# Wider rows in a routing table, a shorter start for VectorE, a store behind weight loads, and two PSUM banks for one pair

## Chip, cores, metric

The kernel runs on one core of a Trainium2 chip. The metric is the device time of one execution in microseconds. TensorE multiplies matrices, VectorE and ScalarE work on what it leaves in PSUM, GpSimd (POOL) makes masks and indices and issues some transfers, and SyncE (SP) issues most of them.

## What is computed

Three layers follow one another: attention with a local window and 32 global tokens, a routed layer of eight experts, and a dense gated layer on all 2176 tokens.

```python
s_ll = scale * np.matmul(q_l, k_l.transpose(0, 1, 3, 2))
s_ll = np.where(np.abs(pos[:, None] - pos[None, :]) <= 32, s_ll, -1000000000.0)
s_l = np.concatenate([s_lg, s_ll], axis=-1)       # 512 local queries, 32 global keys
out_l = np.matmul(sm(s_l), np.concatenate([v_g, v_l], axis=2))
out_g = np.matmul(sm(s_g), v_all)                 # 32 global queries see all keys
...
do_compute = x @ w_skip > 0                       # the others keep x
e_idx = np.argmax(xc @ w_gate, axis=1)
y[mask] = gate_w[mask, None] * (np.maximum(xc[mask] @ w1[e], 0.0) @ w2[e])
out[do_compute] = xc + y
...
return ((x @ w_a) * (x @ w_b) @ w_out).astype(np.float32)
```

There are 4 batches of 8 heads of size 64; the model width is 512, an expert's inner width 1024, the dense layer's 1536. All is float32.

## The kernel before

**Attention** (to some 131 us of the trace) works on 16 pairs of heads, four to a batch. `pair(p)` issues, on every engine, pieces of several pairs: scores S of pair p+2 (`emit_S`, `sps`), their masked maxima M on VectorE (`emit_M`, tiles `sm` and `nm`), exponentials E on ScalarE (L986), transposes T of the next pair (`tps`, `tpg`, copied to `pt`, `ptg`), values PV of pair p (`emit_PV`, into `o`), then X (`emit_X`): the copy `ot` of `o` is multiplied by `xi`, an identity with the router's weights beside it, back into the same PSUM tile `o`, and VectorE writes the token rows `xt` and the logits `lg`. A `slot` may bring a step of the global queries (`emit_G`: `gps`, `gtp`, `gop`); the table `GSTEPS` says in which slots. `pend` holds transfers, and each `tick` after a group of matmuls lets one be issued: keys and queries (`raw`), values (`vt`), stores of `x2d`, sixteen writes of zeros to `xs` (`zero_xs`), and the first weights of the experts. `start()` issues S, M and E of pairs 0 and 1 and T of pair 0, with `idle(n)` putting n matmuls on constants (`zp<-zb`) between them. `last_pairs` is the end of it, pairs 14 and 15, in which the experts' first steps already begin.

**Routing.** Every token gets a slot in the table `xs` in DRAM, 256 rows and more for each expert; a row is 512 floats of the token, a gate weight and the token's number, `ROW` = 514 floats. POOL scatters the rows of `xt` (four tiles a batch) and of `xg` (the global tokens) by an indirect transfer. Rows that no token fills keep what `zero_xs` wrote. `load_row` reads 128 rows of `xs` for an expert.

**Experts** (132 to 276 us) go through the work items of `WORK`, four steps to each. A step needs two loads of weights of 512 KB (`fetch(i)`: a part of `w1` and one of `w2`, tiles `raw`), which ScalarE and VectorE split into a high and a low part (`hi`, `lo`); `layer1` makes `ph`, ScalarE's `hr` is turned in `turn_h` (`pt`), `layer2` sums into `acc`. All weights, rows and stores of `x2d` are issued by SP in one order, written out below L1600: weights of steps 4 to 6, then `st.store_last()` (the four stores of the last batch's tokens), then `st.fetch(7)`, then the rows of the third item, and from there weights seven steps ahead.

**The dense layer** (276 to 690 us) adds its result up in the output; the last tile is done in two halves of 256 columns, each stored as soon as VectorE has it (L560).

Of the kernel before, what the change touches and what calls it, by code (L numbers as in the profile page):

```python
# [27 lines left out]
ROW = 514  # L28
REG = NTOK
# [26 lines left out]
          (2, 0): (32, 37, 38), (2, 1): (40, 45, 46), (3, 0): (43, 49, 54), (3, 1): (48, 53, 57)}  # L56
# [8 lines left out]
def moe_stack_kernel(ctx: ExitStack, tc: tile.TileContext, qk, v, gq, w9, w1, w2, wa, wb, wo, out):  # L65
# [5 lines left out]
    xs = dram.tile([E * REG, ROW], F32, name="xs")  # L71
# [17 lines left out]
class State:  # L89
# [66 lines left out]
    def load_row(self, k, t, xr, scat):  # L156
        r = self.tc.nc.sync.dma_start(xr, self.xs[bass.ds(self.expert(k) * REG + 128 * (WORK[k][1] + t), 128), :])
        after(self.tc, r, scat)
# [92 lines left out]
class Late:  # L251
# [286 lines left out]
    def second(self, b, g):  # L538

        nc = self.nc  # L540
        for q, t in enumerate(self.TILES[b]):
# [8 lines left out]
            for c in halves:  # L550
# [7 lines left out]
                if g == self.NM // 2 - 1:  # L558
                    nc.vector.tensor_tensor(o[:, c], acc[:, c], o[:, c], ALU.add)
                    nc.sync.dma_start(dst[:, c], o[:, c])  # L560
# [265 lines left out]
def attention_and_routing(tc, const, ident, qk, v, gq, w9, x2d, xs, st_):  # L826
    nc = tc.nc
    with ExitStack() as st:
# [14 lines left out]
        xg = c1.tile([128, ROW], F32, name="xg")  # L843
# [11 lines left out]
        zrow = c1.tile([128, ROW], F32, name="zrow")  # L855
# [64 lines left out]
        nc.gpsimd.memset(masks[64:128, 2, 96:128], -1e30)  # L920
        nc.gpsimd.memset(zrow, 0.0)
# [19 lines left out]

        nc.vector.tensor_copy(xg[:, 513:514].bitcast(I32), tokid[:, 16:17])
        nc.vector.tensor_copy(base, pb8)
# [73 lines left out]
        def emit_PV(p):  # L1017

            o = oxs[p] = ps_o.tile([128, 2, 512], F32, tag="o", name="o")
            vt = vts[p]  # L1020
            for j in range(2):
                for k in range(2):
                    r = slice(64 * k, 64 * k + 64)
                    for hh in range(2):
                        c = slice(64 * hh, 64 * hh + 64)
                        mm = nc.tensor.matmul(o[c, k, 128 * j:128 * j + 128], lhsT=vt[r, WIN, c], rhs=pts[p, 2][r, j, :],
                                              start=(j == 0), stop=False, skip_group_check=True)
            tick(mm)
            for i in range(4):
                k, j = divmod(i, 2)  # L1030
                for w in range(2):
                    c = slice(64 * w, 64 * w + 64)
                    for hh in range(2):
                        r = slice(64 * hh, 64 * hh + 64)
                        mm = nc.tensor.matmul(o[r, k, 128 * j + 64 * w:128 * j + 64 * w + 64], lhsT=vt[:, 2 * i + w, r],  # L1035
# [4 lines left out]
            st_.ot = nc.scalar.activation(ot.rearrange("p k j q -> p k (j q)"), o[:, :, 0:256], AF.Copy).ins  # L1040
# [9 lines left out]
        def emit_X(p):  # L1050
            b, hp = divmod(p, 4)
            if hp == 0:
                xt[b] = x_p.tile([128, 4, ROW], F32, tag="xt", name="xt")
                lg[b] = r_p.tile([128, 4, 6, 9], F32, tag="lg", name="lg")
                lgp[b] = r_p.tile([128, 4, 3, 9], F32, tag="lgp", name="lgp")
            o, ot = oxs.pop(p), ots.pop(p)
            for k in range(2):
                for j in range(2):
                    mm = nc.tensor.matmul(o[:, k, 146 * j:146 * j + 146], lhsT=ot[:, k, j, :], rhs=xi[:, hp, :], start=True, stop=True)  # L1059
            tick(mm)  # L1060
            xp = o[:, :, 0:292].rearrange("p k (j h c) -> p k j h c", j=2, h=2)
            ld = lg[b][:, :, 2 * hp:2 * hp + 2, :] if hp < 3 else lgp[b][:, :, 1:3, :]
            nc.vector.tensor_tensor(ld.rearrange("p (k j) h e -> p k j h e", k=2), xp[:, :, :, :, 64:73],
                                    dens[p][:, :, :, :, None].to_broadcast([128, 2, 2, 2, 9]), ALU.mult)
# [7 lines left out]
            def tokens():  # L1072
                nc.vector.tensor_tensor(
                    xt[b][:, :, 128 * hp:128 * hp + 128].rearrange("p (k j) (h d) -> p k j h d", k=2, h=2),
                    xp[:, :, :, :, 0:64],
                    dens[p][:, :, :, :, None].to_broadcast([128, 2, 2, 2, 64]), ALU.mult)
# [296 lines left out]
        def start():  # L1373
            nc.vector.memset(xi[0:64, :, 73:146], 0.0)
            nc.vector.memset(xi[64:128, :, 0:73], 0.0)
            for hp in range(4):
                nc.vector.tensor_copy(xi[0:64, hp, 0:64], ident[0:64, 0:64])
                nc.vector.tensor_copy(xi[64:128, hp, 73:137], ident[64:128, 64:128])
# [5 lines left out]
            nc.scalar.dma_start(w9s, w9.rearrange("a p e -> p a e"))  # L1384
            for g in gpts:
# [13 lines left out]
            idle(4)  # L1399
            emit_T(0)  # L1400
            emit_M(1, 1)

# [9 lines left out]
def experts(tc, const, dram, ident, w1, w2, x2d, xs, st, late):  # L1412
    nc = tc.nc
    with ExitStack() as es:
# [190 lines left out]
        for i in range(4, 7):  # L1605
            st.fetch(i, (1,) if i < 6 else (0, 1))
        st.store_last()
        st.fetch(7)
# [224 lines left out]
```

## Time and profile before

| | |
|---|---|
| time, median of 3 runs | 704.7 us (703.27 to 707.7) |
| the profiled execution, as timed | 698.71 us |
| its span, first to last instruction | 696.9 us |
| TensorE busy | 674.1 us, 97% |
| VectorE, ScalarE, POOL busy | 490.6, 397.0, 130.8 us |
| mean granted TensorE clock | 0.996 |
| DMA | 154.86 MB, 222 GB/s in the mean |

The span is what the trace covers; the timed figure of the same execution has 1.8 us around it. The median of the timed runs lies 6 us above that execution, so a stretch read from the trace counts as a difference, not as a share of the median. [...] Busy times are sums over stages that differ: attention waits for vectors, scalars and transfers, the two later stages for TensorE.

### The profile page before, as it was taken

To read this page: it belongs to the slowest core of one execution; us is meant where nothing else is said; L and a number is where in the kernel's file an instruction comes from. 1 tells how busy PE (TensorE), PEld (TensorE's weight loads), DVE (VectorE), ACT (ScalarE), POOL (GpSimd) and SP (SyncE) were. 2 spreads that over 40 slices of the span, in tenths; PEclk is the share of its full clock that TensorE was granted. 3 is DMA by queue.
4 is the path that set the end of the run, shared out by engine and by line. 5 is a ranking of instruction groups with operands and counts; after the bars stand their busy time and mean duration, and the time that the engine had idled before them with its cause. 6 is when DMAs were issued, how large, how long until landed. Compare 5 with 4: busy or idle time off the path is not lost.

```text
span 696.9 us, 16731 instructions
## 1 busy us (share of the span) xinstructions
PE 674.1 (97%) x6329; PEld 604.6 (87%) x6329; DVE 490.6 (70%) x1278; ACT 397.0 (57%) x973; POOL 130.8 (19%) x213
## 2 busy tenths in 40 slices
PE   8898999989999999999999999999999999999996
PEld 5777887868998888879999999999999999999995
DVE  5667878986968999967975796856375656544444
ACT  5667778865857884567467554544454544443220
POOL 4002213130101210010111122312231232212000
PEclk9999999999999999999999999999999999999999
DMA  8898778799999936632785589996599679549853
GB/s 282 219 233 281 240 222 280 229 310 361 371 369 346 346 121 228 219 134 92 226 333 128 77 188 327 313 221 119 65 268 216 121 151 327 75 61 213 288 179 111
DMA packets 86141, 154.86 MB, mean 222 GB/s; under 512 B 8663, under 2 KB 40279, under 8 KB 84516
## 3 DMA queue, kind: packets, MB, share of 16 engines
q1 hardware_dynamic: 69236, 110.80, 49.1%
q0 software_dynamic: 15744, 42.87, 27.5%
q8 instruction: 52, 0.85, 0.5%
q14 instruction: 37, 0.30, 0.1%
q10 hardware_dynamic: 1072, 0.04, 0.1%
HBM read 105.95 MB, written 51.18 MB: 225 GB/s over the span
## 4 chain that ended last, share of the span: by engine, by line
PE 80%; ACT 3%; DMA 3%; DVE 3%; issue 1%; POOL 0%; SPq 0%; DVEq 0%; POOLq 0%
PE bank L527 32%; PE bank L557 19%; PE acc L1516 8%; PE ph L243 6%; PE bank L583 3%; DMA raw<-w 3%; PE ph L235 2%; PE o L1059 1%; PE sps L963 1%; PE bank L462 1%; PE pt L1502 1%; ACT sm L986 1%; PE o L1035 1%; PE tps L1000 1%; PE tp L204 1%
## 5 line engine op out<-in xcount | busy, mean ns | idle before, releaser
L527 PE MATMUL bank<-xh,w 128*128 128x256 f32 (+1 forms) x1232 | 251.4, 290 | 0.1
L527 PEld LDWEIGHTS bank<-xh,w 128*128 128x128 f32 x1232 | 200.5, 189 | 4.2 <-DVE tmp L649 0.4
L527 PE MATMUL bank<-xl,w 128*128 128x256 f32 (+1 forms) x616 | 178.4, 290 | 0.0
L557 PE MATMUL bank<-woh,g 128*128 128x512 f32 (+1 forms) x412 | 143.7, 392 | 1.2 <-ACT o L563 0.5
L527 PEld LDWEIGHTS bank<-xl,w 128*128 128x128 f32 x616 | 116.1, 188 | 4.2
L181 DVE TENSOR_TENSOR lo<-raw,hi 128x1024 fp32r<-128x1024 f32 x72 | 87.0, 1221 | 11.9 <-ACT hi L171 10.8
L557 PEld LDWEIGHTS bank<-woh,g 128*128 128x128 f32 x412 | 77.3, 188 | 15.6 <-ACT o L563 1.0
L557 PE MATMUL bank<-wol,g 128*128 128x512 f32 (+1 forms) x206 | 80.4, 390 | 0.0
L171 ACT ACTIVATE hi<-raw 128x1024 fp32r<-128x1024 f32 x72 | 75.4, 1054 | 7.8 <-PE acc L1516 4.4
L607 ACT ACTIVATE g<-tmp 128x256 fp32r<-128x256 f32 (+1 forms) x88 | 37.8, 431 | 69.7 <-DVE tmp L649 68.9
L564 POOL DMA_DIRECT2D out<-raw x48 | 39.1, 815 | 141.6 <-ACT raw L563 127.0
L639 DVE TENSOR_TENSOR tmp<-bank,tmp 128x256 f32<-128x256 f32 (+1 forms) x44 | 18.8, 440 | 58.5 <-PE bank L527 58.4
L563 ACT ACTIVATE raw<-bank 128x512 f32<-128x512 f32 x48 | 28.6, 595 | 51.6 <-PE bank L557 50.5
L986 ACT ACTIVATE sm<-sm,nm 128x160 f32<-128x160 f32 x128 | 52.9, 419 | 7.8 <-DVE nm L975 7.8
L564 POOL DMA_DIRECT2D out<-o x37 | 29.6, 801 | 139.2 <-ACT o L563 101.7
L607 ACT ACTIVATE tmp<-bank 128x256 f32<-128x256 f32 (+1 forms) x88 | 34.6, 400 | 25.7 <-PE bank L527 22.2
L649 DVE TENSOR_TENSOR tmp<-bank,tmp 128x256 f32<-128x256 f32 (+1 forms) x88 | 38.9, 442 | 11.7 <-PE bank L527 10.2
L557 PEld LDWEIGHTS bank<-wol,g 128*128 128x128 f32 x206 | 38.7, 188 | 4.6
L645 DVE TENSOR_TENSOR g<-tmp,g 128x256 fp32r<-128x256 f32 (+1 forms) x88 | 38.3, 437 | 3.1 <-ACT g L607 1.4
L563 ACT ACTIVATE o<-bank 128x512 f32<-128x512 f32 x37 | 21.9, 596 | 31.9 <-PE bank L557 29.9
L243 PE MATMUL ph<-hi,xh 128*128 128x256 f32 x132 | 40.0, 303 | 0.0
L243 PE MATMUL ph<-hi,xl 128*128 128x256 f32 x132 | 37.5, 284 | 0.0
(265 smaller groups left out, 1276.5 us busy)
## 6 DMA issues: line engine op xcount, KB each, us to landing
raw<-w SPq DMA_DIRECT2D x64, 512.0 KB
out<-raw POOLq DMA_DIRECT2D x48, 256.0 KB, 4.6
out<-o POOLq DMA_DIRECT2D x37, 256.0 KB, 4.5
raw<-qk SPq DMA_DIRECT2D x28, 272.0 KB
xr<-x2d SPq DMA_DIRECT2D x25, 256.0 KB
raw<-wa SPq DMA_DIRECT2D x12, 512.0 KB
raw<-wb SPq DMA_DIRECT2D x12, 512.0 KB
raw<-wo SPq DMA_DIRECT2D x12, 512.0 KB
```

What stands on the lines that cost most here:

```text
L171: nc.scalar.activation(hi, rv, AF.Copy)
L181: nc.vector.tensor_tensor(lo, rv, hi.bitcast(F32), ALU.subtract)
L243: nc.tensor.matmul(ph, lhsT=x[:, d, :], rhs=w[:, d, :], start=(z == 0), stop=(z == 11))
L527: self.nc.tensor.matmul(bank[:, 0:n], lhsT=w[:, k], rhs=x[:, xp, k], start=start and z == 0, stop=z == 5, skip_group_check=not start)
L557: nc.tensor.matmul(acc[:, c], lhsT=a, rhs=w[:, c], start=(j == 0 and z == 0), stop=(j == 1 and z == 2))
L563: nc.scalar.activation(o, acc, AF.Copy)
L564: i = nc.gpsimd.dma_start(dst, o, accum_op=ALU.add if g else ALU.bypass)
L607: cp = lambda o, i: nc.scalar.activation(o, i, AF.Copy)
L645: tt(g4[2 * j + 1][:, h], (u, p)[h][j], g4[2 * j].bitcast(F32)[:, h], ALU.subtract)
L649: tt(v, (b1, b2)[h][j][:, 0:n], v, ALU.mult)
L986: st_.exp = nc.scalar.activation(sm, sm, AF.Exp, bias=nm[:, hh, j:j + 1], scale=-1.0, accum_out=dens[p][:, k, j, hh:hh + 1]).ins
L1516: nc.tensor.matmul(acc, lhsT=a[:, j, c], rhs=w[:, j, :], start=(q == 0 and z == 0), stop=(q == NQ - 1 and z == 5))
```

## The change

Six edits are made at once.

Rows of `xs` are 528 floats apart (`PITCH`) in place of 514; the zero row, `xg` and `xt` are as wide, with the pad filled on POOL, and `load_row` still reads 514 floats of each row. In `start()` eight copies into `xi` go from VectorE to ScalarE, two copies that read POOL's token numbers go behind the maxima of pair 1, and `idle(4)` is left out. `st.store_last()` is issued behind `st.fetch(7)`. PV of pair 14 writes two tiles of one bank each from the pool of the score tiles, and its copies and products are split in two. One global step's transposes, of (3, 0), move from slot 49 to slot 51, from before the values of pair 12 to before its X. The last tile's second half is stored from ScalarE's queue.

```diff
--- before.py
+++ after.py
@@ -26,6 +26,7 @@
 ROW = 514
+PITCH = 528
 REG = NTOK
@@ -53,7 +54,7 @@
 GSTEPS = {(0, 0): (3, 5, 6), (0, 1): (8, 13, 14), (1, 0): (16, 21, 22), (1, 1): (24, 29, 30),
-          (2, 0): (32, 37, 38), (2, 1): (40, 45, 46), (3, 0): (43, 49, 54), (3, 1): (48, 53, 57)}
+          (2, 0): (32, 37, 38), (2, 1): (40, 45, 46), (3, 0): (43, 51, 54), (3, 1): (48, 53, 57)}
@@ -68,7 +69,7 @@
     x2d = dram.tile([NTOK, DM], F32, name="x2d")
-    xs = dram.tile([E * REG, ROW], F32, name="xs")
+    xs = dram.tile([E * REG, PITCH], F32, name="xs")
@@ -154,7 +155,7 @@
     def load_row(self, k, t, xr, scat):
-        r = self.tc.nc.sync.dma_start(xr, self.xs[bass.ds(self.expert(k) * REG + 128 * (WORK[k][1] + t), 128), :])
+        r = self.tc.nc.sync.dma_start(xr, self.xs[bass.ds(self.expert(k) * REG + 128 * (WORK[k][1] + t), 128), 0:ROW])
         after(self.tc, r, scat)
@@ -557,7 +558,7 @@
                     nc.vector.tensor_tensor(o[:, c], acc[:, c], o[:, c], ALU.add)
-                    nc.sync.dma_start(dst[:, c], o[:, c])
+                    (nc.scalar if c.start else nc.sync).dma_start(dst[:, c], o[:, c])
             if g < self.NM // 2 - 1:
@@ -840,7 +841,7 @@
-        xg = c1.tile([128, ROW], F32, name="xg")
+        xg = c1.tile([128, PITCH], F32, name="xg")
         sp = c1.tile([128, NT, 18], F32, name="sp")
@@ -852,7 +853,7 @@
         masks = c1.tile([128, 3, 160], F32, name="masks")
-        zrow = c1.tile([128, ROW], F32, name="zrow")
+        zrow = c1.tile([128, PITCH], F32, name="zrow")
         gq_sb = c1.tile([128, B, H, SG], F32, name="gq_sb")
@@ -918,6 +919,7 @@
         nc.gpsimd.memset(masks[64:128, 2, 96:128], -1e30)
+        nc.gpsimd.memset(xg[:, ROW:], 0.0)
         nc.gpsimd.memset(zrow, 0.0)
@@ -938,9 +940,6 @@
             nc.gpsimd.iota(tokid[32 * b:32 * b + 32, NT - 1:NT], pattern=[[0, 1]], base=b * (SL + SG), channel_multiplier=1)
-
-        nc.vector.tensor_copy(xg[:, 513:514].bitcast(I32), tokid[:, 16:17])
-        nc.vector.tensor_copy(base, pb8)
@@ -1016,14 +1015,19 @@
-            o = oxs[p] = ps_o.tile([128, 2, 512], F32, tag="o", name="o")
+            if p == NPAIR - 2:
+                both, o = None, [ps_s.tile([128, 512], F32, tag="s", name="o2") for k in range(2)]
+            else:
+                both = ps_o.tile([128, 2, 512], F32, tag="o", name="o")
+                o = [both[:, k] for k in range(2)]
+            oxs[p] = both, o
             vt = vts[p]
...
                         c = slice(64 * hh, 64 * hh + 64)
-                        mm = nc.tensor.matmul(o[c, k, 128 * j:128 * j + 128], lhsT=vt[r, WIN, c], rhs=pts[p, 2][r, j, :],
+                        mm = nc.tensor.matmul(o[k][c, 128 * j:128 * j + 128], lhsT=vt[r, WIN, c], rhs=pts[p, 2][r, j, :],
                                               start=(j == 0), stop=False, skip_group_check=True)
@@ -1032,12 +1036,17 @@
                         r = slice(64 * hh, 64 * hh + 64)
-                        mm = nc.tensor.matmul(o[r, k, 128 * j + 64 * w:128 * j + 64 * w + 64], lhsT=vt[:, 2 * i + w, r],
+                        mm = nc.tensor.matmul(o[k][r, 128 * j + 64 * w:128 * j + 64 * w + 64], lhsT=vt[:, 2 * i + w, r],
                                               rhs=pts[p, hh][:, i, c], start=False, stop=True, skip_group_check=True)
...
             ot = ots[p] = ot_p.tile([128, 2, 2, 128], F32, tag="ot", name="ot")
-            st_.ot = nc.scalar.activation(ot.rearrange("p k j q -> p k (j q)"), o[:, :, 0:256], AF.Copy).ins
+            of = ot.rearrange("p k j q -> p k (j q)")
+            if both is None:
+                for k in range(2):
+                    st_.ot = nc.scalar.activation(of[:, k], o[k][:, 0:256], AF.Copy).ins
+            else:
+                st_.ot = nc.scalar.activation(of, both[:, :, 0:256], AF.Copy).ins
@@ -1050,18 +1059,21 @@
             if hp == 0:
-                xt[b] = x_p.tile([128, 4, ROW], F32, tag="xt", name="xt")
+                xt[b] = x_p.tile([128, 4, PITCH], F32, tag="xt", name="xt")
+                nc.gpsimd.memset(xt[b][:, :, ROW:], 0.0)
                 lg[b] = r_p.tile([128, 4, 6, 9], F32, tag="lg", name="lg")
                 lgp[b] = r_p.tile([128, 4, 3, 9], F32, tag="lgp", name="lgp")
-            o, ot = oxs.pop(p), ots.pop(p)
+            (both, o), ot = oxs.pop(p), ots.pop(p)
             for k in range(2):
                 for j in range(2):
-                    mm = nc.tensor.matmul(o[:, k, 146 * j:146 * j + 146], lhsT=ot[:, k, j, :], rhs=xi[:, hp, :], start=True, stop=True)
+                    mm = nc.tensor.matmul(o[k][:, 146 * j:146 * j + 146], lhsT=ot[:, k, j, :], rhs=xi[:, hp, :], start=True, stop=True)
             tick(mm)
-            xp = o[:, :, 0:292].rearrange("p k (j h c) -> p k j h c", j=2, h=2)
+            parts = [(slice(0, 2), both[:, :, 0:292])] if both is not None else [(slice(k, k + 1), o[k][:, None, 0:292]) for k in range(2)]
+            xps = [(k, x.rearrange("p k (j h c) -> p k j h c", j=2, h=2)) for k, x in parts]
             ld = lg[b][:, :, 2 * hp:2 * hp + 2, :] if hp < 3 else lgp[b][:, :, 1:3, :]
-            nc.vector.tensor_tensor(ld.rearrange("p (k j) h e -> p k j h e", k=2), xp[:, :, :, :, 64:73],
-                                    dens[p][:, :, :, :, None].to_broadcast([128, 2, 2, 2, 9]), ALU.mult)
+            for k, xp in xps:
+                nc.vector.tensor_tensor(ld.rearrange("p (k j) h e -> p k j h e", k=2)[:, k], xp[:, :, :, :, 64:73],
+                                        dens[p][:, k, :, :, None].to_broadcast([128, k.stop - k.start, 2, 2, 9]), ALU.mult)
             if hp == 1:
@@ -1070,10 +1082,10 @@
             def tokens():
-                nc.vector.tensor_tensor(
-                    xt[b][:, :, 128 * hp:128 * hp + 128].rearrange("p (k j) (h d) -> p k j h d", k=2, h=2),
-                    xp[:, :, :, :, 0:64],
-                    dens[p][:, :, :, :, None].to_broadcast([128, 2, 2, 2, 64]), ALU.mult)
+                xv = xt[b][:, :, 128 * hp:128 * hp + 128].rearrange("p (k j) (h d) -> p k j h d", k=2, h=2)
+                for k, xp in xps:
+                    nc.vector.tensor_tensor(xv[:, k], xp[:, :, :, :, 0:64],
+                                            dens[p][:, k, :, :, None].to_broadcast([128, k.stop - k.start, 2, 2, 64]), ALU.mult)
                 sums()
@@ -1373,15 +1385,15 @@
             nc.vector.memset(xi[64:128, :, 0:73], 0.0)
-            for hp in range(4):
-                nc.vector.tensor_copy(xi[0:64, hp, 0:64], ident[0:64, 0:64])
-                nc.vector.tensor_copy(xi[64:128, hp, 73:137], ident[64:128, 64:128])
             for s in range(2):
...
             nc.scalar.dma_start(w9s, w9.rearrange("a p e -> p a e"))
+            for hp in range(4):
+                nc.scalar.activation(xi[0:64, hp, 0:64], ident[0:64, 0:64], AF.Copy)
+                nc.scalar.activation(xi[64:128, hp, 73:137], ident[64:128, 64:128], AF.Copy)
             for g in gpts:
@@ -1396,9 +1408,10 @@
             emit_E(1, 0)
-            idle(4)
             emit_T(0)
             emit_M(1, 1)
+            nc.vector.tensor_copy(xg[:, 513:514].bitcast(I32), tokid[:, 16:17])
+            nc.vector.tensor_copy(base, pb8)
@@ -1604,8 +1617,8 @@
             st.fetch(i, (1,) if i < 6 else (0, 1))
+        st.fetch(7)
         st.store_last()
-        st.fetch(7)
         load_rows(2)
```

SyncE's order around the last batch's stores, before (`raw<-w` are the weights, a step's two loads being `128x4x256` and `128x2x512`; the ISA rows set registers):

```order
L152 DMA raw<-w 128x4x256
L152 ISA
L152 DMA raw<-w 128x2x512
L1264 DMA x2d<-xt 128x512 x4
L152 ISA
L152 DMA raw<-w 128x4x256
L152 ISA
L152 DMA raw<-w 128x2x512
L157 ISA
L157 DMA xr<-xs 128x514
```

and after:

```order
L153 DMA raw<-w 128x4x256
L153 ISA
L153 DMA raw<-w 128x2x512
L153 ISA
L153 DMA raw<-w 128x4x256
L153 ISA
L153 DMA raw<-w 128x2x512
L1276 DMA x2d<-xt 128x512 x4
L158 ISA
L158 DMA xr<-xs 128x514
```

The four stores stand behind both loads of step 7 and right ahead of the loads of the rows `xr`.

VectorE's first work, before, from the copy of `base` (the copy `xg<-tokid` stands just ahead of it) to the first maximum of pair 0 (`sm,nm<-sps`):

```order
L943 COPY base<-pb_137 128x8
L1374 MEMSET xi 64x4x73
L1375 MEMSET xi 64x4x73
L1377 COPY xi<-ident 64x64
L1378 COPY xi<-ident 64x64
L1377 COPY xi<-ident 64x64
L1378 COPY xi<-ident 64x64
L1377 COPY xi<-ident 64x64
L1378 COPY xi<-ident 64x64
L1377 COPY xi<-ident 64x64
L1378 COPY xi<-ident 64x64
L975 ISA sm_224,nm<-sps,masks 128x160
```

and after:

```order
L906 MEMSET run 128x8
L1386 MEMSET xi 64x4x73
L1387 MEMSET xi 64x4x73
L974 ISA sm_223,nm<-sps,masks 128x160
L974 ISA nm 128x1
```

Two fills are all that is left ahead of the maximum; both copies stand after the sixteenth maximum, and the eight of `xi` on ScalarE ahead of its first exponential.

TensorE around the values of pair 14 (`o<-ptg,vt` and `o<-pt,vt`), before, from those values on:

```order
L1026 MATMUL o<-ptg,vt 64x128 x8
L1035 MATMUL o<-pt,vt 64x64 x16
L1127 MATMUL gop<-vt,gpt_141 32x64 x20
L1000 MATMUL tps<-ident,sm_225 128x128 x8
L1010 MATMUL tpg<-ident,smg_227 128x128 x2
L1059 MATMUL o<-xi,ot 128x146 x4
L1142 MATMUL ltp<-ident,xg 128x128 x4
L204 MATMUL eps<-ident,row 128x128 x4
```

and after, where the names carry buffer numbers since there are two tiles:

```order
L1030 MATMUL o_2757<-ptg,vt 64x128 x2
L1030 MATMUL o_2758<-ptg,vt 64x128 x2
L1030 MATMUL o_2757<-ptg,vt 64x128 x2
L1030 MATMUL o_2758<-ptg,vt 64x128 x2
L1039 MATMUL o_2757<-pt,vt 64x64 x8
L1039 MATMUL o_2758<-pt,vt 64x64 x8
L1139 MATMUL gop<-vt,gpt_141 32x64 x20
L999 MATMUL tps<-ident,sm_224 128x128 x8
L1009 MATMUL tpg<-ident,smg_226 128x128 x2
L1069 MATMUL o_2757<-xi,ot 128x146 x2
L1069 MATMUL o_2758<-xi,ot 128x146 x2
L1154 MATMUL ltp<-ident,xg 128x128 x4
```

The same matmuls go to two tiles, `o_2757` and `o_2758`, and the X product of pair 13 ahead of them no longer shares a tile with them.

## Rows read from the trace of the kernel before

**Rows 1.** The page, first part: busy us (share of span) by engine.
```profile
PE 674.1 (97%) x6329; PEld 604.6 (87%) x6329; DVE 490.6 (70%) x1278; ACT 397.0 (57%) x973; POOL 130.8 (19%) x213
```

**Rows 2.** The waits of PE: us in total, times, longest us.
```profile
PE pt L1502 <- ACT hr L247: 3.5, 2, 3.3
...
PE o L1026 <- DVE xt L1073: 1.2, 1, 1.2
```

**Rows 3.** Windows: us, busy us by engine, PEclk, DMA share, GB/s.
```profile
20.00:60.00 40.00, 35.60 (x853) 30.48 (x853) 27.84 (x156) 27.45 (x108) 3.06 (x11) 1.00 1.00 258
60.00:100.00 40.00, 38.51 (x925) 32.72 (x927) 31.88 (x172) 31.38 (x121) 9.80 (x20) 1.00 0.71 229
40.00:42.00 2.00, 1.82 (x60) 1.49 (x60) 1.04 (x10) 1.01 (x5) 0.29 (x1) 1.00 1.11 148
54.00:56.00 2.00, 1.72 (x53) 1.43 (x43) 2.00 (x10) 2.00 (x11) 0.29 (x1) 1.00 1.07 402
120.40:127.10 6.70, 5.50 (x115) 4.98 (x114) 5.87 (x13) 6.40 (x22) 2.26 (x5) 1.00 0.47 136
156.00:158.00 2.00, 2.00 (x7) 1.61 (x7) 1.59 (x2) 0.38 (x1) 0.00 (x0) 0.50 1.04 266
```

**Rows 4.** Timeline of PE, 30 to 60 us: start, us, operation [idle].
```profile
33.26 0.65 PE L1026 MATMUL o<-ptg,vt 64*64 64x128 f32 x10 [1.72 <-issue]
```

**Rows 5.** The chain of waits, 100 to 165 us: start, us, what.
```profile
140.91 11.69 DMA raw<-w
...
156.38 2.42 PE acc L1516 x6
...
160.90 1.40 PE acc L1516 x6
```

**Rows 6.** Timeline of ACT, 146 to 162 us.
```profile
152.63 1.06 ACT L171 ACTIVATE hi<-raw 128x1024 fp32r<-128x1024 f32 x1 [3.35 <-DMA raw<-w]
```

**Rows 7.** Timeline of SP, 128 to 171 us: DMA issues, not transfers.
```profile
136.35 3.52 SPq L1264 DMA_DIRECT2D x2d<-xt  x4
...
151.88 2.13 SPq L157 DMA_DIRECT2D xr<-xs  x2
154.26 16.06 SPq L152 DMA_DIRECT2D raw<-w  x14
```

**Rows 8.** DMA view, 140 to 150 us: packets, MB, share of engines.
```profile
q1 hardware_dynamic: 1829, 2.71, 79.3%
```

**Rows 9.** The tile view of `xs`, its last line.
```profile
DMA to landing us min/median/max: 2.6/4.3/8.8
```

**Rows 10.** Timeline of SP, 24 to 60 us.
```profile
35.02 2.14 SPq L927 DMA_DIRECT2D xs<-zrow  x3
...
50.79 3.41 SPq L1264 DMA_DIRECT2D x2d<-xt  x4
```

**Rows 11.** Timeline of all engines, 2 to 16 us.
```profile
1.72 2.16 SPq L870 DMA_DIRECT2D raw<-qk  x4
...
7.15 0.15 DVE L942 COPY xg<-tokid 128x1 int32<-128x1 int32 x1 [5.94 <-POOL tokid L940]
...
7.18 0.80 SPq L870 DMA_DIRECT2D raw<-qk  x2
...
8.40 0.87 PE L963 MATMUL sps<-raw 64*64 64x128 f32 x32 [0.21 <-DMA raw<-qk]
...
10.36 1.35 PE L963 MATMUL sps<-raw 64*64 64x128 f32 x32 [1.09 <-DVE nm L975]
...
11.65 1.04 PE L1371 MATMUL zp<-zb 128*128 128x512 bf16 x4
...
14.28 1.54 PE L963 MATMUL sps<-raw 64*64 64x128 f32 x64
```

**Rows 12.** Timeline of all engines, 688 to 697 us.
```profile
688.13 3.84 SPq L560 DMA_DIRECT2D out<-raw  x4
...
690.15 0.42 DVE L559 TENSOR_TENSOR raw<-bank,raw 128x256 f32<-128x256 f32 x1 [0.25 <-PE bank L557]
```

## Prediction

> **What bounds the kernel now.** I read the totals first, then the waits of TensorE, then stretches of the attention stage, then the chain of waits where the largest wait lies. TensorE is busy for 674.1 of the 696.9 us [rows 1], so this change can win only what TensorE idles, what it does at a low clock, and the two ends of the program. The mean says little about where; three places do.
>
> First, one wait of 3.3 us for `hr` of ScalarE (L247) [rows 2]. The chain shows it is not ScalarE's: a load of expert weights issued at 140.91 lands 11.69 us later [rows 5], and ScalarE's copy `hi` sits idle for 3.35 us until then [rows 6]. Two microseconds after it, the granted clock is 0.50 (1.2 GHz) over 156 to 158, where elsewhere in the rows it is 1.00 (2.4 GHz) [rows 3]; the first six `acc` matmuls behind the stall take 2.42 us, the next six of the kind 1.40 [rows 5].
>
> Second, the attention from 20 to 60 us leaves TensorE idle for 40 − 35.60 = 4.40 us, from 60 to 100 only 40 − 38.51 = 1.49 [rows 3]. The largest single gap, 1.72 us before PV at 33.26, has no releaser among the engines [rows 4]; PV also needs values that DMA brings. The DMA share is 1.00 in the first stretch and 0.71 in the second [rows 3].
>
> Third, the start: the second S waits 1.09 us for VectorE's maxima and is followed by 1.04 us of filler matmuls [rows 11].
>
> **Store behind the weights (term A).** SyncE issues four stores of `x2d` of 256 KB in 3.52 us from 136.35, and only then the two loads of weight step 7 [rows 7]. In 140 to 150 us SyncE's queue moved 2.71 MB in 10 us [rows 8], 0.27 MB/us, so the 1.05 MB of stores that now stand behind cost the load about 3.9 us. Landing at 152.6 − 3.9 = 148.7, it is there before ScalarE asks at 152.63 − 3.35 = 149.28 [rows 6]: the wait of 3.3 us goes. The low clock came after it and nothing else here differs, so I count its 2.42 − 1.40 = 1.02 us too: 4.3 together.
>
> What is late next? The rows of the third work item are issued at 151.88 [rows 7], after the scatter, and come no earlier; TensorE turns them just ahead of the `acc` at 160.90 [rows 5], after the change about 156.6. Transfers at this table land 2.6 to 4.3 us (least and median) after their issue [rows 9], 154.5 to 156.2: just in time. Of the queues passed, SyncE alone is touched: behind the four stores now stand the row loads and the fourteen weight loads of 154.26 [rows 7]; these take 16.06/14 × 2 = 2.3 us for a step of two, less than the 160.90 − 156.38 = 4.5 us that this stalled step took or the 3 us I estimate for an undisturbed one, so SyncE catches up. The weight loads of steps 8 and up cannot be earlier than that row load, so their slack shrinks by the 4.3 us that TensorE wins. I take 4.0, with 2 (half the gain eaten by step 8's weights) and 4.8 (more matmuls ran at the low clock than those six) as ends.
>
> **Wider rows (term B).** Sixteen writes of zeros, 257 KB each and 2056 bytes a row, go to `xs` up to 60 us, and with 528 floats a row is 2112 bytes, 64-byte steps from row to row rather than 8. In 40 to 42 us, with the writes of 35.02 [rows 10] still draining, the DMA engines' share is 1.11 and yet they move 148 GB/s; in 54 to 56, with four stores of 2048-byte rows issued at 50.79 [rows 10], the share is 1.07 and they move 402 [rows 3]. So something about these rows keeps the engines occupied 2.7 times as long a byte, and their start address is the one thing the edit changes. If the writes ran at 402, one of 0.263 MB would take 0.65 us instead of 1.78, and 16 of them give back 18 us of transfer time in a stage where the share is full. What TensorE can take of it is its idle time: the second stretch, without zeros, shows 1.49 us left over, so 4.40 − 1.49 = 2.9 us. Ends: 0 (the pitch is not the reason) and 4.4 (no gap left).
>
> Rows [rows 3, 10] show the slow writes but not their cause. [...]
>
> The pads cost POOL some small fills: `xg`'s once, `xt`'s once a batch, four in 131 us; nobody on the critical path waits for POOL there, so 0. The scatters carry 2.7% more bytes: 0.
>
> **First maxima (term C).** VectorE's first work waited until 7.15 for POOL's token numbers, 5.94 us [rows 11]; two copies that need them move behind the maxima of pair 1 and eight more go to ScalarE, idle till then. So pair 0's maxima start about when S ends, some 4 us earlier; the 1.09 us wait and the filler's 1.04 go: 2.1 us by engines alone. The keys of pair 2 may not follow: their loads are issued at 7.18 to 7.98, and pair 1's, issued by 1.72 + 2.16 = 3.88, were awaited until 8.40, 4.5 us [rows 11]. The same delay gives 12.5 to 12.9, against S(2) at 14.28: 1.4 us, ends 0 and 2.1. With the moved copies VectorE loses nothing, since they stand where it waits for T.
>
> **Own banks, global step, last store (D, E).** PV of pair 14 waited 1.2 us for VectorE's `xt` [rows 2], its bank's last reader; with two own banks that wait goes. But ScalarE is busy 6.40 of the 6.70 us around it [rows 3], and the next X needs ScalarE's copy `ot`, now in two instructions. So I take 0.3, ends −0.3 and 1.2; moving step 3,0's transposes behind T(13) only reorders ScalarE's work there and is in that term. At the end SyncE issues four stores in 3.84 us from 688.13, 0.96 each, so the last would begin at 691.0, while its data is ready at 690.15 + 0.42 = 690.57 [rows 12]: on ScalarE's idle queue 0.4 us earlier, ends 0 and 0.6.
>
> **Sum.** 4.0 + 2.9 + 1.4 + 0.3 + 0.4 = 9.0 us off the profiled execution's span of 696.9 (698.71 us as timed). Set against the median of 704.7, which is 6 us above that execution, it gives 695.7. What a measurement of this kernel can tell from no change is about 1%, 7 us.
>
> **Rivals.** (1) *The pitch does nothing.* [...] Against it: the rates above. B is 0, and if the DMA stays full then half of C goes with it: 704.7 − (4.0 + 0.7 + 0.3 + 0.4) = 699.3. Chance 0.28.
>
> (2) *The stall moves.* Stores, row loads and step 8's weights are all issued later relative to TensorE; if ScalarE stops for step 8 instead of 7, A falls to 1.5, the clock dip included: 704.7 − 6.5 = 698.2. For it: row loads that are issued only at 151.88 [rows 7]. Against it: 2.3 us of supply a step against 3 of use. Chance 0.14.
>
> (3) *Slower: the clock falls in the first pairs.* Without the four filler matmuls TensorE idles about 1 us ahead of S(2), at a point where DMA feeds it late. The gap of 1.72 us at 33.26 brought no fall (clock 1.00 over 20 to 60 [rows 3, 4]), the one of 3.3 did. If the fall comes once, it costs 1 us or so; if it recurs in each of the first six pairs, with six matmuls' worth of 1.02 and their neighbours' share, some 1.7 us a pair by estimate, that is 10 us, and B and C are lost with it: 704.7 − 4.7 + 10 = 710. It decides from three pairs on (4.7 / 1.7). Chance 0.05.
>
> **How the numbers follow.** The forecast has 0.5; its own ends, with A to E at odds, are 691 to 698. Something between, such as C lost alone, has the rest, 0.03. The range of 691 to 700.5 holds the forecast and most of rivals 1 and 2 and leaves out rival 3 and the tails. Faster by over 1% is below 697.7: 0.45 of the forecast, 0.06 of rival 1, 0.05 of rival 2: 0.56. Slower by over 1% is above 711.7: 0.02 of rival 3, and 0.02 for a wait I have not seen: 0.04. Within 1%: 0.40.
>
> **What would show it.** A right: no wait of TensorE for `hr` above 1 us, no 0.50 clock behind 156. B right: with the zeros in flight DMA moves 300 GB/s and more, and 20 to 60 us holds above 38 us of TensorE's work. C right: VectorE's first maximum before 6 us, S(2) near 12.9. D: PV of pair 14 waits for ScalarE, not `xt`. E: the last store issued near 690.6. The prediction is wrong if the zeros drain at 150 GB/s as before, or if a wait of 2 us or more stands at step 8 or 9.

## The result and the profile after

| | before | changed |
|---|---|---|
| median, 4 runs each | 703.99 us (703.25 to 707.7) | 696.97 us (695.35 to 698.1) |
| ratio to before | | 0.9893, 95% interval 0.9862 to 0.9925 |
| profiled execution, as timed | 698.71 us | 696.35 us |

The kernel became 1.07% faster, some 7.5 us, with an interval of 5 to 10 us. The forecast was 9.0 us less, 695.7. The two traces differ by less, 696.9 against 694.6 us of span; the experiments show why.

The page of the changed kernel, first part and part 3 (instruction queue: packets, MB, share):

```profile
PE 673.8 (97%) x6323; PEld 603.8 (87%) x6325; DVE 489.3 (70%) x1272; ACT 399.8 (58%) x982; POOL 131.5 (19%) x218
...
q8 instruction: 52, 0.85, 0.5%
```

TensorE is busy as long as before [rows 1]. Windows of its trace (as in rows 3, with TensorE's busy time alone), the first three against theirs, the last two for what follows:

```profile
20.00:60.00 40.00, 38.88 (x1001) 1.00 0.87 287
60.00:100.00 40.00, 37.18 (x865) 1.00 0.70 217
40.00:42.00 2.00, 2.00 (x44) 1.00 0.99 341
150.00:154.00 4.00, 4.00 (x28) 1.00 0.34 104
155.00:195.00 40.00, 38.07 (x251) 1.00 1.06 369
```

From 20 to 60 us TensorE idles 1.1 us in place of 4.4; and 40 to 42 us, with writes of zeros from 38.93 on under way, moves 341 GB/s at a share of 0.99. From 60 to 100 it idles 2.8 in place of 1.5; whether the change does that is for the experiments. The start, all engines (against rows 11), and the end (against rows 12):

```profile
5.99 0.32 DVE L974 CUSTOM_DVE_ANT_0 sm<-sps,masks 128x160 f32<-128x160 f32 x1 [4.08 <-PE sps L962]
...
11.51 1.66 PE L962 MATMUL sps<-raw 64*64 64x128 f32 x55
...
14.51 0.66 PE L1030 MATMUL o<-ptg,vt 64*64 64x128 f32 x15 [1.17 <-issue]
```

```profile
687.83 0.42 DVE L560 TENSOR_TENSOR raw<-bank,raw 128x256 f32<-128x256 f32 x1 [0.26 <-PE bank L558]
688.29 0.37 ACTq L561 DMA_DIRECT2D out<-raw  x1
```

VectorE's first maximum is 3.7 us earlier (9.73 before), S(2) 2.8 us, more than the 1.4 foreseen, but PV(0) then pauses 1.17 us for "issue", and PV of pair 1 starts 1.44 us earlier than before (21.85, then 23.29). At the end the last store goes out 0.04 us after its data; yet the span ends 6.35 us after that data's last operation, where it ended 6.33 after it before, so term E is not to be seen.

The weights of step 7: the chain runs through without a wait where rows 5 had one, and TensorE keeps its clock (1.00 from 150 to 195 us).

```profile
153.27 0.22 PE pt L1515 x2
...
155.01 0.44 PE tp L205 x4
155.44 1.39 PE acc L1529 x6
```

But TensorE's waits (against rows 2) have two new lines. Pauses on "issue" come up below; of the other the timeline shows the place:

```profile
PE tp L205 <- DMA xr<-xs: 1.9, 1, 1.9
PE gop L1139 <- issue: 1.9, 4, 0.5
```

```profile
179.40 1.34 PE L205 MATMUL tp<-ident,xr 128*128 128x128 f32 x8 [1.90 <-DMA xr<-xs]
```

The rows of the fifth work item come 1.9 us late at 179. SyncE's issues (against rows 7):

```profile
138.01 3.03 SPq L1276 DMA_DIRECT2D x2d<-xt  x4
149.80 3.65 SPq L158 DMA_DIRECT2D xr<-xs  x2
153.66 15.71 SPq L153 DMA_DIRECT2D raw<-w  x14
169.57 2.04 SPq L158 DMA_DIRECT2D xr<-xs  x2
```

The rows needed at 177.5 were issued at 169.57, behind fourteen weight loads that take 15.71 us to issue, as before (16.06), and DMA is full from 155 on (share 1.06 in the windows above).

### The profile page after: what moved, and what is told of

Read it like the earlier page. It is cut to its first block, busy times and chain, and to the rows that moved or that the text cites. A ratio compares the mean times of both kernels' runs of the same rounds, so it can differ in the third digit from the quotient of the medians.

```text
span 694.6 us, 16735 instructions
## 1 busy us (share of the span) xinstructions
PE 673.8 (97%) x6323; PEld 603.8 (87%) x6325; DVE 489.3 (70%) x1272; ACT 399.8 (58%) x982; POOL 131.5 (19%) x218
## 4 chain that ended last, share of the span: by engine, by line
PE 79%; ACT 4%; DVE 3%; DMA 2%; issue 1%; SPq 0%; POOL 0%; POOLq 0%; ACTq 0%; DVEq 0%
PE bank L528 32%; PE bank L558 19%; PE acc L1529 8%; PE ph L244 6%; PE bank L584 2%; PE ph L236 2%; ACT sm L985 1%; DMA xr<-xs 1%; PE o L1069 1%; PE pt L1515 1%; PE sps L962 1%; PE bank L463 1%; DMA xr<-x2d 1%; PE tp L205 1%; PE o L1039 1%
## 5 line engine op out<-in xcount | busy, mean ns | idle before, releaser
L974 DVE CUSTOM_DVE_ANT_0 sm<-sps,masks 128x160 f32<-128x160 f32 x128 | 32.6, 320 | 6.6 <-PE sps L962 6.4
```

## The experiments

Ratios are to the kernel before, timed on the same chip; absolute times differ by chip (medians of the kernel before: 699.2, 704.4 and 697.9 us for the three sets), so ratios are what is compared. The whole change was timed for the first result and beside p1, s1 and b1; set against u1 to u4 and d1 to f1 it is compared across chips.

| run | what stands of the change | ratio, 95% interval |
|---|---|---|
| first result | all | 0.9893 (0.9862 to 0.9925) |
| c1_changed_again | all | 0.9899 (0.9845 to 0.9953) |
| u1_pitch514 | all but the pitch | 0.9968 (0.9942 to 0.9993) |
| u2_store_first | all but the store's place | 0.9878 (0.9850 to 0.9907) |
| u3_start_old | all but the start | 0.9922 (0.9892 to 0.9951) |
| u4_banks_gstep_old | all but banks and global step | 0.9906 (0.9869 to 0.9943) |
| p1_pitch_only | the pitch | 0.9944 (0.9918 to 0.9970) |
| s1_swap_only | the store's place | 1.0011 (0.9980 to 1.0042) |
| b1_pitch_start_store | pitch, start, last store | 0.9914 (0.9890 to 0.9938) |
| d1_more_slow_rows | all, and 12 writes of 514-float rows | 0.9957 (0.9929 to 0.9985) |
| d2_more_even_rows | all, and 12 writes of 528-float rows | 0.9939 (0.9915 to 0.9962) |
| f1_fill_gap | all, and step 8's weights earlier | 0.9876 (0.9853 to 0.9898) |

**The pitch.** Undone alone (and the fills of the pads with it):

```diff
-PITCH = 528
+PITCH = 514
```

> The changed kernel with rows of the table 514 floats apart again; all else as changed (697.0 us). Theory 1, the terms add up as predicted: the zero writes drain at about 150 GB/s again, TensorE idles some 3 us more between 20 and 60 us, and the time is 2.9 us more, 699.9 (0 to 4.4 more). Theory 2, attention's end is set elsewhere: in the changed kernel's trace the values of pair 6 start 5.8 us earlier than before, but attention ends at 132.1 in both traces, so what the pitch gains is given back by 131 us; the time stays within 1 us of 697.0 and the slow stretch 20 to 60 shows all the same.

The first theory held. The ratio goes from 0.9893 to 0.9968: 0.75%, 5 us, uncertain by some 3, so its 2.9 us are within it. Two windows of its trace, and the DMA view from 18 to 60 us of this kernel and then of the changed one (queue: packets, MB, share of 16 engines):

```profile
20.00:60.00 40.00, 35.03 (x873) 1.00 1.02 274
38.00:40.00 2.00, 1.65 (x64) 1.00 1.18 116
```

```profile
q1 hardware_dynamic: 5726, 10.91, 96.3%
```

```profile
q1 hardware_dynamic: 5947, 11.44, 82.2%
```

With 2056-byte rows the queue is busy for 96.3% of the time with 10.91 MB, with 2112 for 82.2% with 11.44: 19% less engine time a byte, in spite of the pads. A stretch of 116 GB/s at a share of 1.18 is back. By the trace's records of single packets from 18 to 60 us, those of 2056 bytes take 134 ns on average and up to 1533, those of 2112 bytes 89 and up to 239; the loads beside them (2176 bytes) take 140 in the first case and 110 in the second. The other way round:

> The kernel before with rows of 528 floats and the pads, nothing else. Theory P, the pitch carries most of it, by 20 to 60 us, where TensorE waits at every 256th of its instructions for code that is late behind the zero writes: 3 to 5 us less, ratio 0.993 to 0.996, TensorE busy 38 us or more from 20 to 60, no pause there above 0.8 us. Theory S, the sum as predicted: 2.9 us less, and the wait for step 7's weights is still 3.3 us.

The ratio is 0.9944, 3.9 us (2.1 to 5.8), which holds theory S's 2.9 too; but its wait of 3.3 us for step 7's weights is not in the trace, where the longest is 1.3. TensorE's share of the two stretches moves as in the whole change (compare rows 3):

```profile
20.00:60.00 40.00, 38.73 (x946) 1.00 0.84 278
60.00:100.00 40.00, 36.75 (x877) 1.00 0.66 210
```

**What waits behind the slow rows: code.** The larger pauses while the zeros are written are put to "issue". In the kernel with 514 floats:

```profile
31.45 0.44 PE L1029 MATMUL o<-ptg,vt 64*64 64x128 f32 x6 [1.30 <-issue]
...
49.85 0.22 PE L1205 MATMUL cp<-oh,ones 128*128 128x24 bf16 x3 [2.26 <-issue]
```

At the pause that ends at 31.45, 6 matmuls of PV(2)'s first kind are left; in the kernel before, the one of 1.72 us came with 10 left [rows 4]. The kernel before has four more filler matmuls ahead. Taking windows from 0 to a point inside each pause (the kernel before, then this one, then u3_start_old, which has the fillers again and pauses with 10 left), the counts are the same:

```profile
0.00:33.00 33.00, 28.19 (x597) 20.88 (x597) 19.56 (x114) 20.59 (x80) 8.42 (x53) 1.00 0.86 251
```

```profile
0.00:31.00 31.00, 27.51 (x597) 21.57 (x597) 18.12 (x108) 21.87 (x84) 8.37 (x53) 1.00 0.89 261
```

```profile
0.00:32.00 32.00, 28.64 (x597) 21.38 (x597) 19.53 (x114) 19.75 (x76) 8.57 (x55) 1.00 0.79 260
```

```profile
32.54 0.65 PE L1033 MATMUL o<-ptg,vt 64*64 64x128 f32 x10 [1.18 <-issue]
```

597 matmuls and 597 weight loads come ahead of the pause in all three, though it is another matmul: the place is set by the number of instructions. Counted in the trace's records with TensorE's semaphore instructions, pauses of this sort in these and the later traces come at 449, 961, 1217, 1729, 1985, 2241, 2497, 3009, 3265, 4033 and 4289 (one or two less where records are missing), always 193 over a multiple of 256. Part 3 of the page shows transfers of instructions (queue q8), 52 of 0.85 MB in all, 16 KB each; the first trace after holds 12789 records of TensorE's instructions, close to 50 times 256 (12800).

That TensorE waits for its own code is read from this and from the records of q8's packets, which show the arrival too. The k-th of them goes with instruction 256k + 193: in none of the 14 traces does TensorE pass such a place within 1 us after the end of that packet, and 47 pauses of over 0.25 us at these places end 1.2 to 1.6 us after it, but for four with rows of 514 floats (1.9 to 2.2). For the pause of 2.26 us at 49.85 the packet starts at 45.67; the DMA view of 45 to 46 us shows it as 12.4% of 16 engines' microsecond, that is 1.99 us, and TensorE goes on 2.19 us after the packet's end:

```profile
q8 instruction: 1, 0.02, 12.4%
```

Two limits. Not every pause on "issue" is one: that of 1.12 us at 40.77 in this trace (0.42 in the trace before) comes at instruction 1635, and five of 0.4 us near instruction 4289 (in the first trace after, c1, p1, s1 and b1) end 4.7 us or more after their packet; their cause stays open. And wide rows do not end the waits for code: f1_fill_gap and d3_three_pitches pause 2.0 and 2.3 us at instruction 961,

```profile
26.01 0.27 PE L1139 MATMUL gop<-vt,gpt 128*32 128x64 f32 x2 [2.00 <-issue]
```

and idle 3.3 and 3.8 us from 20 to 60, where the other nine traces with wide rows idle 0.8 to 1.9 and the three with narrow ones 3.7 to 5.0.

> The changed kernel with the eight copies of xi and the two moved copies ahead of VectorE's maxima again and the four filler matmuls back. Theory 1: 1.4 us more, 698.4. Theory 2, attention's end is set elsewhere: values of pairs 0 to 6 start 1.5 us later, attention ends at the same time, 697.0 within 1.

```diff
+                nc.vector.tensor_copy(xi[0:64, hp, 0:64], ident[0:64, 0:64])
...
-                nc.scalar.activation(xi[0:64, hp, 0:64], ident[0:64, 0:64], AF.Copy)
...
             emit_E(1, 0)
+            idle(4)
             emit_T(0)
```

Start undone (the two copies that read the token numbers go back too): 0.9922 against 0.9893 and 0.9899, 0.2 to 0.3%, 2 us, within the intervals; PV of pair 1 starts at 23.4 as before. The second theory of these two runs, that attention's end is set elsewhere, fell: on the same chip PV of pair 15 starts at 123.4 and 122.7 in u2 and u4, which have both pitch and start, at 125.3 in this kernel and at 126.1 in u1_pitch514. In these traces what is won early arrives at the end.

To load DMA where it had room, twelve writes of zeros were added to the changed kernel in pairs 6, 7 and 9 (`xd` is a table of their own):

```diff
+            if p in (6, 7, 9):
+                n = 4 * (6, 7, 9).index(p)
+                pend.extend(lambda z=z: nc.sync.dma_start(st_.xd[128 * z:128 * z + 128, :], zrow[:, 0:ROW]) for z in range(n, n + 4))
```

> The changed kernel with twelve more writes of zeros, 128 rows of 514 floats each, to a table of their own that nothing reads, four in each of pairs 6, 7 and 9, where DMA has room (share 0.70 from 60 to 100). Theory P, rows of 2056 bytes keep the DMA engines and delay TensorE's code at every 256th instruction: TensorE's idle time from 60 to 100 grows by 1 us or more against the next run, with pauses at instructions of 193 over a multiple of 256. Rival: slow rows cost only where the DMA share is at 1.00; then both runs are alike and near the changed kernel.

> The same twelve writes with rows of 528 floats. Theory P: each lands in the time of a store of x2d, TensorE from 60 to 100 as in the changed kernel within 0.5 us, and the kernel is 1 us or more faster than the last. Rival, the row's start on a multiple of 256 bytes decides: as slow as the last.

The window 60 to 100, the landing of the writes (us from issue: least, median, most) and the larger pauses, first with 514 floats, then with 528:

```profile
60.00:100.00 40.00, 35.08 (x842) 1.00 0.97 302
```

```profile
DMA to landing us min/median/max: 6.9/7.8/8.1
```

```profile
74.18 0.24 PE L964 MATMUL sps<-raw 64*64 64x32 f32 x1 [1.66 <-issue]
...
89.98 0.68 PE L1041 MATMUL o<-pt,vt 128*64 128x64 f32 x14 [0.76 <-issue]
...
97.74 0.30 PE L964 MATMUL sps<-raw 64*64 64x32 f32 x3 [1.87 <-issue]
```

```profile
60.00:100.00 40.00, 35.49 (x849) 1.00 0.92 304
```

```profile
DMA to landing us min/median/max: 5.5/6.1/6.2
```

```profile
74.02 0.24 PE L964 MATMUL sps<-raw 64*64 64x32 f32 x1 [2.17 <-issue]
...
97.32 0.30 PE L964 MATMUL sps<-raw 64*64 64x32 f32 x3 [1.59 <-issue]
```

Both have pauses of 1.6 to 2.2 us at instructions 3265 and 4289 that the changed kernel lacks (its share there is 0.70), and f1_fill_gap, on the same chip without these writes, has none and idles 1.3 us there: with more transfer of either kind code came late here. The narrow rows land 1.7 us later and add the pause at 89.98 (instruction 4033) and one of 0.6 us at 3009. TensorE idles 4.9 and 4.5 us in the window, 0.4 apart where 1 was expected; by ratio the two are 0.18% apart, less than the intervals, and their medians are the same (695.3). So the narrow rows' own price outside a full stretch is not settled. The rival's "near the changed kernel" does not hold: both are 0.6 to 0.8% above f1_fill_gap on one chip, with intervals apart; that run's own edit (0.2% by the ratios, 0.3 to 0.4% by its trace, below) explains a part.

> The same with four writes each of rows of 516 (pair 6), 520 (pair 7) and 576 floats (pair 9), to see from which pitch on a row is fast: 2064 bytes are a multiple of 16, 2080 of 32, 2304 of 256. If 32 bytes are the unit, 516 lands late (as 514) and 520 early (as 528); if 64 are, 520 is late too; if 256, 576 alone lands faster than 528.

```diff
+            w = {6: 516, 7: 520, 9: 576}.get(p)
+            if w:
+                pend.extend(lambda z=z, w=w: nc.sync.dma_start(st_.xd[w][128 * z:128 * z + 128, :], zwide[:, 0:w]) for z in range(4))
```

Landing times (5.2, 6.7 and 4.1 us) are of pairs with different transfers beside them and decide nothing. The trace's records of the packets say more, pair against pair, 512 packets each (mean, longest in ns):

| pair | d1, 2056 bytes | d3 | d2, 2112 bytes |
|---|---|---|---|
| 6 | 125, 709 | 2064 bytes: 103, 802 | 90, 238 |
| 7 | 105, 441 | 2080 bytes: 90, 289 | 88, 228 |
| 9 | 90, 308 | 2304 bytes: 96, 254 | 89, 233 |

So the long packets are there with a pitch of 2056 and 2064 and gone with 2080: a multiple of 32 bytes is enough here, as far as one execution shows. Pair 9 tells nothing of 2304, since even rows of 2056 are hardly slower there. Start and length of a row change together, so which of the two counts stays open.

**The store behind the weights.**

> The changed kernel with the four stores ahead of the weights of step 7 again. Both theories: the wait of TensorE for the weights of step 7 comes back, about 3 us, with the low clock behind it; by the sum 4.0 us more, 701.0. What tells more: in the changed trace the rows of the fifth item come 1.9 us late at 179 us; if that is the price of the new order (SyncE's row loads stand behind stores and weights), it goes here, and the net is 2 to 3 us more, 699.5.

```diff
-        st.fetch(7)
         st.store_last()
+        st.fetch(7)
```

> The kernel before with the weights of step 7 ahead of the four stores, nothing else. Theory S, as predicted: 4.0 us less, ratio 0.994. Rival 2 of the prediction, the stall moves: the wait of 3.3 us goes and a wait of about 2 us for the rows of the fifth item takes its place, 1 to 3 us less, ratio 0.996 to 0.999; the last run, in which undoing the swap cost nothing, speaks for it.

Undone it costs nothing (0.9878), alone it gives nothing (1.0011). TensorE's waits say how: of u2_store_first, then of p1_pitch_only (both with the stores ahead), then of s1_swap_only (behind):

```profile
PE pt L1515 <- ACT hr L248: 1.1, 1, 1.1
PE tp L205 <- DMA xr<-xs: 0.9, 1, 0.9
```

```profile
PE pt L1517 <- ACT hr L248: 1.6, 2, 1.3
...
PE tp L205 <- DMA xr<-xs: 0.6, 1, 0.6
```

```profile
PE tp L204 <- DMA xr<-xs: 2.0, 1, 2.0
PE gps L1100 <- issue: 2.0, 1, 2.0
```

With the stores ahead, weights and rows together make TensorE wait 1.1 + 0.9 and 1.6 + 0.6 us; with them behind, the rows alone 2.0 (1.9 to 2.0 in u1, u3, u4 and c1 as well). The wait only changes its place. (The second line of s1 is a wait for code, at instruction 1729, with rows of 514 floats.) From the last X product to the dense layer's first matmul the three traces u2, p1 and b1, with the stores ahead, take 144.0 to 144.2 us, and the traces with them behind 144.1 to 146.8. The 3.3 us of the trace before [rows 2], which takes 146.8 there, were not met again: no other trace with that order had more than 1.3 at once. All three of these have wide rows, so whether the rows or the one execution made the difference is not shown. The low clock can follow the new wait as well: in u4, d1 and d2 the granted clock is 0.50 right behind the rows' wait, in the others it is not. In u4, whose wait ends at 174.1:

```profile
175.00:177.00 2.00, 2.00 (x7) 0.50 1.06 383
```

The traces suggest the cause of the rows' wait: SyncE stands from 149.80 at rows that wait for the scatter, DMA idles (150 to 154: share 0.34), and then all is full. So the weights of step 8 were put ahead of those rows, and VectorE works out the experts' order `sidi` one step earlier, which their address needs:

```diff
         st.store_last()
-        load_rows(2)
...
+            if i == NQ:
+                st.fetch(8)
+                load_rows(2)
...
-            if i in (3, 4, 7, 8):
+            if i in (2, 3, 7, 8):
                 some(3)
```

> The changed kernel with SyncE's order changed once more: the weights of step 8 ahead of the rows of the third item, and for that the experts' order (sidi) worked out one step earlier on VectorE. In the traces DMA is nearly idle from 151 to 154 us, while SyncE stands at those rows, and at a share of 1.05 to 1.07 from 155 to 195, where the rows of the fifth item come 1.9 to 2.0 us late. Theory: the first items are held by the bytes that DMA moves; then the gap is filled, the rows' wait shrinks by 1 to 2 us and the time by as much (ratio 0.987). Rival: it is the order alone, and another wait of the same size takes its place (ratio 0.989 to 0.990).

```profile
150.00:154.00 4.00, 3.02 (x21) 1.00 0.99 313
155.00:195.00 40.00, 40.00 (x270) 1.00 1.07 372
```

```profile
PE tp L205 <- DMA xr<-xs: 1.0, 1, 1.0
```

The gap is filled (share 0.99 from 150 to 154), the wait is 1.0 us and now for the third item's rows, and from 155 to 195 TensorE never idles, where it idled 1.9 us. From the last X product to the dense layer this trace takes 144.1 us, those of d1 to d3 on the same chip 145.9 to 146.8, but the first trace after 144.2. The ratio, 0.9876, is 1 to 2 us better than the whole change's on other chips, as expected, with overlapping intervals; by the medians of its set the kernel is 7.5 us below the kernel before, as in the first result. So it beats the kernel before; that it beats the changed one is not shown.

**Banks and global step; all but these and the store.**

> The changed kernel with pair 14 in the shared bank and the global step (3, 0) in slot 49 again. Theory 1: 0.3 us more (0.3 less to 1.2 more). Theory 2 in its first form, the moved step is what gives attention's gain back (in the changed trace pairs 12 to 14 take 1.8, 1.2 and 1.0 us longer each than before): attention ends 3 to 4 us earlier than 132.1 and the time falls to 693 to 694. In its second form, it is the DMA or the pipeline's order, and the end stays at 132.

> The changed kernel with the four stores ahead again, pair 14 in the shared bank and the global step in slot 49: pitch, start and last store alone. If the swap and the banks are worth nothing, the ratio is 0.988 to 0.989, as that of the whole change or a little better; by the sum as predicted it is 4.3 us slower than the whole, 0.995.

> The changed kernel itself once more, beside the parts of it on one chip. Expected ratio to the kernel before 0.989 as measured first. Its trace tells whether the slow stretch of 113 to 119 us of the first trace (TensorE pausing three times for 0.4 to 0.5 us while DMA was nearly idle, attention's end at 132.1) belongs to the kernel (then it is there again) or to that execution (then attention ends at 126 to 128, as in the variants of the last runs).

The edit of u4_banks_gstep_old (b1_pitch_start_store has it too, with the stores ahead again; c1_changed_again is the changed kernel as it is):

```diff
-          (2, 0): (32, 37, 38), (2, 1): (40, 45, 46), (3, 0): (43, 51, 54), (3, 1): (48, 53, 57)}
+          (2, 0): (32, 37, 38), (2, 1): (40, 45, 46), (3, 0): (43, 49, 54), (3, 1): (48, 53, 57)}
...
-            if p == NPAIR - 2:
+            if p == -1:
```

Undoing banks and step gives 0.9906, 0.1% more than 0.9893: nothing that these runs can tell from zero. Leaving out both them and the store gives 0.9914, 0.15% above c1_changed_again: the same. The second theory's first form falls: on one chip PV of pair 15 starts at 122.7 without banks and step (u4) and at 123.4 with them (u2), 0.7 us apart and not 3 to 4, and u4's time did not fall. Some of it is there: from PV of pair 12 to PV of pair 15 u2 takes 20.1 us and u4 18.6. On the chip of c1 it is the other way, 22.5 with banks and step and 24.1 without (b1), so the traces do not settle what the two are worth. TensorE is busy 39.0 and 39.3 us of 60 to 100 in u4 and u2, so the idle time there in the first trace after is not the change's either. The pauses of 113 to 119 us go with the chip more than with the change: c1_changed_again has them again,

```profile
116.52 0.81 PE L1039 MATMUL o<-pt,vt 128*64 128x64 f32 x19 [0.45 <-issue]
...
118.52 0.31 PE L1139 MATMUL gop<-vt,gpt 128*32 128x64 f32 x4 [0.47 <-issue]
119.27 0.22 PE L1139 MATMUL gop<-vt,gpt 128*32 128x64 f32 x1 [0.44 <-issue]
```

each 0.4 to 0.5 us, at the same place as in the first trace after; p1, s1 and b1, timed on the same chip, have more of them there; u1 to u4, d1 to d3 and f1, on two others, have none, nor has the trace of before. They lie on "issue" too, but not at 193 over a multiple of 256, and with DMA at a share of 0.68 (c1, 114 to 120 us). What they are stays open. They go some way to explain the traces' small difference: the one of before is of an execution without them, 5 us below the median.

## Why the prediction was right

The range and the direction held. That the size came near (9.0 us forecast, 7.5 measured) is in part luck: term A, 4.0 of the 9.0, gave nothing, and the other terms together gave more than their 5.0, within their intervals.

- **Term A, 4.0 us, failed.** It rests on one wait of 3.3 us in one execution; with the stores ahead no other trace has one above 1.3. The step that failed was "What is late next? ... just in time": it followed the third item's rows and SyncE's supply of weights, and stopped at step 8. What is late next is the rows of the fifth item, 25 us on, because DMA is full from 155 to 195 (share 1.06) and swapping two transfers changes no sum of bytes. Measured: 0.8 us slower, interval 1.4 faster to 3.0 slower. That is the prediction's rival 2, whose place (step 8) was wrong; A is nothing rather than its 1.5. What a clock of 0.50 is worth shows in the trace before: matmuls of `ph`, 256 columns each, start 0.21 us apart at 0.50 (155.1 to 156.2 us) and 0.12 apart at 1.00 (159.0 to 160.2).
- **Term B, 2.9 us, held**, and the wider rows did shorten the slow writes: 3.9 us alone (2.1 to 5.8), 5 us when undone (across chips). The stretch from 20 to 60 gave 3.1 to 3.3 us by p1 and by the first trace after, though f1 and d3 show that it varies. The "zeros drain at 300 GB/s" that was to show it came true as 341 in the window named. Two readings were off: the pause of 1.72 us ahead of 33.26 was for code, whose packet ended at 31.09, and not for the values that the prediction had in mind; and the 2.7 times of 40 to 42 us is that of all packets there, 75% of their time that of loads of 2176 bytes, while the rows themselves take 134 ns against 89, 1.5 times. Rival 1, by which B is 0, falls with the 3.9 us. Nor is a start on a multiple of 256 bytes needed, the rival of d2_more_even_rows: neither 2112 nor 2080 is such a multiple, and their packets take 88 to 90 ns in the mean and 289 at most, where rows of 2056 and 2064 bytes in the same two pairs have some of 441 to 802.
- **Term C, 1.4 us, fits, with E**: b1 less p1, which adds start and last store, is 0.30%, 2.1 us against 1.8 forecast; u3 says 2 us; both are within the intervals. The keys did not hold S(2) until 12.9, it began at 11.5; the wait for code at instruction 449 took back part of it.
- **Term D, 0.3 us**: the wait for `xt` at PV of pair 14 is gone from the trace, and the time is not to be told from no change, as said. **E, 0.4 us**: no gain in the trace's end; not timed alone.
- **Rival 3**, the clock: it stays at 1.00 in the changed kernel's 20 to 100 us.

One upon the other on one chip: pitch 3.9, start and last store 2.1, store behind the weights and banks 1.1 make the 7.1 of c1_changed_again. These are differences of successive ratios, each uncertain by 2 to 4 us, so that they add up shows nothing by itself; only the pitch is clear of zero.

## What to carry to other kernels

Rows written to DRAM by the hundred are worth a try with a padded pitch where DMA is full: 2112 bytes (a multiple of 64) beat 2056 here, 89 ns a packet against 134 and 3.9 us of the kernel's time, and 2080 (a multiple of 32) looked as fast in one execution (90 ns where 2056 took 105 in the same pair). In the stretch that DMA filled (share 1.06), moving one transfer ahead of another moved the wait, from 1.1 + 0.9 us to 2.0: look for where the queue stands idle, and try to fill that. Before a term is built on one long wait, see whether a second execution has it. Where TensorE paused here with no engine to explain it, at one of a row of instructions 256 apart and 1.2 to 1.6 us behind the end of a packet of the instruction queue (43 of 47 such pauses), it was read as code that came late.

## What was not expected of the hardware

TensorE's pauses for code come 193 instructions over a multiple of 256 and last up to 2.3 us; 16 of the 18 longer than 1 us have DMA at a share of 0.85 or more in the 3 us ahead of them. Rows of 2064 bytes still have long packets (802 ns against 238 of 2112 in the same pair), rows of 2080 have not (289 against 228). One chip shows a row of pauses in one place of the program with DMA far from full (share 0.68 from 114 to 120 us in c1_changed_again), others don't, and the kernel before differs by 1% between chips (medians from 697.9 to 704.4 us).
